# A cap on loads under way, more room for weights, and a table of importance in the planned start of an attention and mixing kernel

## The chip, the cores and the metric

The kernel runs on one NeuronCore of a Trainium2 chip. The metric is the device time of one execution in microseconds (us). TensorE (PE) multiplies matrices, VectorE (DVE), ScalarE (ACT) and GpSimd (POOL) work on tiles element by element, and SyncE (SP) issues all of the kernel's DMAs. Each engine works through its own list of instructions strictly in the order in which the program was written; semaphores hold an instruction back until what it needs is there.

## The reference

Two parts follow each other. The first is an attention over 8 heads: a pooled attention (queries, keys and values averaged over 4 positions, its result repeated 4 times) plus a local one (each position sees those less than 4 away). The second mixes tokens with two small weights and channels with two larger ones.

```python
q_d = q.reshape(B, H, Sd, 4, D).mean(axis=3)          # k_d, v_d likewise; B=8 H=8 S=576 D=64
out_up = np.repeat(sm_attn(q_d, k_d, v_d), 4, axis=2)
mask = np.abs(pos[:, None] - pos[None, :]) < 4
scores = np.where(mask, scale * q @ k.T, -1e9)
out_local = softmax(scores) @ v
x = (out_up + out_local)                              # as [B, S, 512]
h = relu(x.T @ w_tok1) @ w_tok2                       # tokens: 576 -> 256 -> 576
u = x + h.T
return u + relu(u @ w_ch1) @ w_ch2                    # channels: 512 -> 1536 -> 512
```

The weights arrive as 64-bit floating-point numbers, everything else as 32-bit ones.

## The kernel before

**Tiling.** The 8 batches are worked through one after another. Per batch, the 576 positions are cut into five tiles (four of 128, one of 64) for attention and the first token product, and into two halves of 256 and 320 positions for what follows. The stages and the names that the profile shows are these. Pooled attention, twice per batch for two halves of the heads: `sd` (scores), `pd` (exponentials), `td` and `ptd` (transposed), `ad` (times the summed values `vd`), `od` (the result). Local attention, per position tile: `sc` (scores), `P` (exponentials), `pT` and `pt` (transposed), `av` (times the values), `x` (the tile of the sum). The pooled result enters the local product as extra rows: twelve small DMAs copy `od` into the rows of `vw` that lie below the loaded values (L515), and `av` multiplies with the whole of `vw`. Then the mixing: `xh` (x in two parts), `t1` (the first token product, five pieces, shown as `t<-xh,W`), `hid` (its positive part), `t2` (the second one, four pieces per half, shown as `t<-ident,x` and `t<-W,hid`), `u`, its largest absolute value `um`, and `uh` (u scaled, in two half-precision parts). Last the channel products: `c<-uh,CW` with C1, `h`, and `c<-h,CX` with C2. Each takes three matmuls for every pair of parts, since numbers are kept in two parts.

**Weights.** A weight in 64 bits is loaded as it is and turned into 32 bits on the chip by `to_f32`: a step on ACT (L211), two on POOL (L214, L217) and one on DVE (L222), all in place in the loaded tile except the last, which for C1 and C2 writes the final tile. C1 and C2 have twelve tiles each, W (the two token weights) nine pieces. The DVE step ends the reading of a loaded piece (`(name, "read", i)`), and the next piece that uses the same buffer is loaded after it. C1's pieces have six buffers (`cw`), W's five (`h`, which later hold the channel products' intermediate results). C2's first four loads use the four `qk` buffers, once batch 0's five local tiles have been transposed, and the next four the `vw` buffer, once the last `av` is done.

**Order.** From the third batch on, and for the channel products of all but the first, the order is written out by hand (the loops at the end). The start, up to the end of batch 0 and the first scaled half of batch 1, is put in order by a planner, `drive`. Each stream of work (a Python generator) says before each step which engine it needs, for how long, and what must be made first. The planner keeps a clock for each engine and one for the loads (230 bytes per ns, and 2 us to land), takes the step that can start earliest, advances the clocks, and lets the stream write its instructions. Among steps on the same engine that can start within `PATIENCE` (0.15 us) of the earliest it takes the first stream in the list. Where PE would be idle in the plan, `keep_busy` puts in at most eight filler matmuls (`busy`). The planned times set only the order of the instructions; on the chip they wait for semaphores alone.

**Loads of batch 0.** `load` (L383) issues the four `qk` tiles ahead of the planner. `load_v` (L398) issues the six `vr` tiles at its first step, `weight_loads` (L230) one piece of W or C1 per step, `load_w` (L420) the two halves of `vw`. All of these go on SyncE's queue, in the planned order, and nothing limits how many are under way.

## Time and profile before

| | |
|---|---|
| median of 3 runs | 970.06 us (966.67 to 973.64) |
| the profiled execution | 967.52 us |
| its span, first to last instruction | 965.7 us |
| PE busy | 911.2 us (94%) |
| DVE, ACT, POOL busy | 425.8, 302.6, 205.5 us |
| mean granted TensorE clock | 0.973 |
| moved by DMA | 71.67 MB, 74 GB/s over the span |

The profile is of one execution. Its page gives the busy time of each engine, the span in 40 slices (a digit is the busy share of a slice in tenths), the DMA queues, the chain of work that ended last, and the costliest groups of instructions. A row of the timeline reads: start, length, engine, line, operation, output <- inputs, shapes and count, and in brackets how long the engine was idle ahead of it and what ended that. `issue` means that the engine waited for nothing that the profile shows. `SPq` is SyncE issuing a DMA. Queue q1 carries the kernel's own DMAs, q8 and q14 the engines' instructions.

### The profile page before, as it was taken

What the parts mean: (1) busy time and instruction counts of PE and PEld (TensorE: products, weight loads), DVE (VectorE), ACT (ScalarE), POOL (GpSimd) and SP (SyncE); (2) the same over time, 40 slices, a digit from 0 to 9 for tenths busy, and PEclk for the clock granted to TensorE, in tenths of its full rate; (3) what the DMA queues carried; (4) which work ended last, traced back from release to release, by engine and by line L of the source; (5) the groups of instructions that cost most, each with busy time, mean ns of one, the idle gap of its engine ahead of it and who ended that gap; (6) DMA issues with size and microseconds to landing.
All of it is one profiled execution on the core that took longest, in us unless ns stands there. A gap on an engine that the chain in (4) does not pass through costs nothing.

```text
span 965.7 us, 29160 instructions
## 1 busy us (share of the span) xinstructions
PE 911.2 (94%) x13142; PEld 698.3 (72%) x13150; DVE 425.8 (44%) x982; ACT 302.6 (31%) x675; POOL 205.5 (21%) x301
## 2 busy tenths in 40 slices
PE   6678899999989999999999999999999999999998
PEld 3545576777867777777877777777877778777876
DVE  4676786426343254334443255324443254333221
ACT  2354455214232142223332141322432142322110
POOL 4399960320222002300122002300113000000000
PEclk9597999999999999999999999999999999999999
DMA  9581630620242012500243002500124000000000
GB/s 261 190 288 54 222 73 15 178 74 26 64 144 55 15 30 78 170 8 21 56 133 76 14 27 81 171 1 28 52 90 123 7 23 21 18 1 22 18 12 28
DMA packets 31756, 71.67 MB, mean 74 GB/s; under 512 B 3808, under 2 KB 16608, under 8 KB 31008
## 3 DMA queue, kind: packets, MB, share of 16 engines
q1 hardware_dynamic: 31632, 69.81, 24.0%
q8 instruction: 103, 1.69, 0.8%
q14 instruction: 21, 0.17, 0.1%
HBM read 58.00 MB, written 9.44 MB: 70 GB/s over the span
## 4 chain that ended last, share of the span: by engine, by line
PE 76%; DVE 10%; POOL 4%; ACT 3%; issue 3%; DMA 2%; SPq 1%; ACTq 0%; POOLq 0%; DVEq 0%
PE c L115 51%; PE t L115 11%; PE av L569 3%; PE td L486 2%; PE ad L501 2%; PE t L633 2%; PE pT L556 2%; PE sc L533 1%; DVE r L550 1%; ACT pd L478 1%; DVE uh L679 1%; DMA vr<-in_vr_dram 1%; DVE P L545 1%; DVE mx L544 1%; PE sd L466 1%
## 5 line engine op out<-in xcount | busy, mean ns | idle before, releaser
L115 PE MATMUL c<-uh,CW 128*128 128x256 f16 (+1 forms) x2304 | 305.8, 287 | 1.9 <-DVE h L756 1.6
L115 PE MATMUL c<-h,CX 128*128 128x256 f16 (+1 forms) x2304 | 306.0, 287 | 1.6 <-issue 1.4
L115 PEld LDWEIGHTS <-CW 128*128 128x128 f16 x2304 | 217.3, 98 | 69.3 <-issue 14.1
L115 PEld LDWEIGHTS <-CX 128*128 128x128 f16 x2304 | 216.6, 98 | 62.6 <-issue 3.1
L756 DVE SCALAR_TENSOR_TENSOR h<-c,h 128x256 f16<-128x256 f32 (+1 forms) x192 | 87.6, 457 | 186.7 <-ACT h L754 186.3
L754 ACT ACTIVATE h<-c 128x256 f16<-128x256 f32 (+1 forms) x192 | 78.7, 410 | 227.0 <-PE c L115 226.8
L412 POOL TENSOR_TENSOR vr<-vr 128x256 f32<-128x256 f32 x48 | 37.4, 780 | 381.4 <-DMA vr<-in_vr_dram 373.0
L782 DVE SCALAR_TENSOR_TENSOR u<-c,io,u 128x256 f32<-128x256 f32 (+1 forms) x64 | 32.9, 514 | 117.2 <-PE c L115 117.1
L115 PE MATMUL t<-W,hid 128*128 128x256 f32 (+1 forms) x384 | 69.6, 317 | 1.8 <-DVE W L242 1.7
L115 PE MATMUL t<-xh,W 128*128 128x512 f32 (+1 forms) x240 | 68.8, 422 | 2.2 <-DVE xh L611 2.2
L437 POOL TENSOR_TENSOR qs<-qk 128x288 f32<-128x288 f32 x56 | 40.7, 727 | 113.4 <-DMA qk<-in_qk_dram 109.8
L658 ACT COPY u<-t 128x256 f32<-128x256 f32 (+1 forms) x64 | 25.5, 398 | 118.1 <-PE t L115 97.3
L660 DVE TENSOR_REDUCE umx<-t 128x1 f32<-128x256 f32 (+1 forms) x64 | 29.3, 458 | 70.5 <-ACT u L658 69.1
L115 PEld LDWEIGHTS t<-W,hid 128*128 128x128 f32 x384 | 55.0, 195 | 4.4 <-DVE W L242 1.9
L115 PEld LDWEIGHTS t<-xh,W 128*128 128x128 f32 (+1 forms) x240 | 44.0, 194 | 13.4 <-DVE xh L611 2.7
L611 DVE TENSOR_TENSOR xh<-x,xh 128x512 fp32r<-128x512 f32 (+1 forms) x40 | 30.4, 765 | 52.9 <-ACT xh L609 52.9
L569 PE MATMUL av<-vw,pt 47*32 47x64 f32 x2304 | 37.9, 226 | 7.2 <-DMA vw<-od 3.7
L569 PEld LDWEIGHTS av<-vw,pt 47*32 47x32 f32 x2304 | 28.1, 107 | 19.8 <-issue 8.0
L574 ACT COPY x<-av 128x512 f32<-128x512 f32 (+1 forms) x40 | 23.3, 584 | 55.0 <-PE av L569 50.8
L547 ACT ACTIVATE P<-P 128x304 f32<-128x304 f32 (+1 forms) x40 | 18.1, 456 | 64.7 <-DVE P L545 64.2
L677 ACT ACTIVATE uh<-u,us 128x256 f16<-128x256 f32 (+1 forms) x64 | 29.6, 525 | 27.7 <-DVE us L121 18.7
L533 PE MATMUL sc<-qk 64*32 64x38 f32 x2304 | 31.1, 212 | 4.4 <-issue 2.6
(107 smaller groups left out, 849.2 us busy)
## 6 DMA issues: line engine op xcount, KB each, us to landing
qk<-in_qk_dram SPq DMA_DIRECT2D x32, 579.0 KB
vr<-in_vr_dram SPq DMA_DIRECT2D x48, 256.0 KB
vw<-in_vw_dram SPq DMA_DIRECT2D x16, 702.0 KB
C_raw<-in_c_dram SPq DMA_DIRECT2D x16, 512.0 KB
out_dram<-u SPq DMA_DIRECT2D x32, 160.0 KB
C_raws<-in_c_dram SPq DMA_DIRECT2D x8, 512.0 KB
out_dram<-u SPq DMA_DIRECT2D x32, 128.0 KB
vw<-od SPq DMA_DIRECT2D x96, 24.0 KB
```

Source lines behind the costliest of these rows:

```text
L115: nc.tensor.matmul(ps, lhs(a), rhs(c), start=first and i == 0, stop=last and i == 2, **kw)
L412: nc.gpsimd.tensor_add(t[:, 0:2], t[:, 0:2], t[:, 2:4])
L437: nc.gpsimd.tensor_add(two, x[:, :, 0:2], x[:, :, 2:4])
L533: nc.tensor.matmul(ps[QB * j:QB * j + QB, par, WB * hp:WB * hp + WB], st.qk[hp][p, QB * g:QB * g + QB], st.qk[hp][p, S + QB * g:S + QB * g ...
L569: nc.tensor.matmul(ps[QB * j:QB * j + QB, par, D * hp:D * hp + D], pt[p, hp, QB * j:QB * j + QB], st.vw[p, g, D * COLUMN[hp]:D * COLUMN[hp ...
L611: nc.vector.tensor_tensor(xh[:, 1], xf(t), xh[:, 0].bitcast(F32), ALU.subtract)
L658: nc.scalar.copy(u, ps)
L660: nc.vector.tensor_reduce(umx[ch][:, c:c + 1], ps, axis=AX.X, op=ALU.max, apply_absolute_value=True)
L677: nc.scalar.activation(t[:, 0], st.u[ch][c], AF.Copy, scale=s)
L754: nc.scalar.activation(ht[:, 0], ps, AF.Relu)
L756: nc.vector.scalar_tensor_tensor(ht[:, 1], ps, 0.0, ht[:, 0], ALU.max, ALU.subtract)
L782: nc.vector.scalar_tensor_tensor(us[c], banks[c], io, us[c], ALU.mult, ALU.add)
```

## The change

Five things change, all of them in the planned start.

The loads of batch 0 (`qk`, `vr`, `vw`, and the W and C1 pieces that wait for no buffer) ask `room` first. While the bytes issued and not yet known to have landed, with the new load's, exceed 1.7 million, `room` takes the oldest load and issues a DMA of one word out of its tile into a small tile `seen`. SyncE can issue that DMA only when the load has landed, so what comes behind it on SyncE waits too. The planner's clocks move on to that load's planned arrival.

The last four of W's nine pieces get four buffers of their own (`wr`), so none of W's loads waits for another piece to be read. The space comes from the scratch for descriptors written by software, set to 1024 bytes.

Each stream gets a name (its group's letter and a number) and a place in `ORDER`. Among the steps on the earliest step's engine within `PATIENCE`, the planner now takes the one that stands first in `ORDER`. In SyncE's case the names that matter at the start are L1 (`vr`), L2 (W), L3 (`vw`), L4 (C1) and L5 (C2).

The six `vr` loads of batch 0 become six steps, and batch 1's five become five, instead of one step for all; batch 1's first still waits for the mixing of batch 0.

The steps of the second token product wait for all four of its weight pieces by name, and the copies of `od` for both of its halves, as the order among them is no longer fixed.

```diff
+ORDER = ("C5 m1 C2 C0 U0 A6 T0 A0 U1 W0 W6 W5 M3 W3 A2 M2 C8 A4 m3 L1 W4 L5 U2 M0 A3 C9 D9 A1 Q0 S0 D11 C7 D4 "
+         "a2 C11 m0 D10 a1 W8 P0 W1 W7 L0 m2 D8 h0 a5 D0 M1 W2 a4 D5 L4 H0 C10 C3 a6 A5 L2 C6 D7 a0 C4 D2 a3 "
+         "C1 P1 D1 D6 D3 L3 ").split()
+UNDER_WAY = 1.7e6
...
+    def room(nbytes):
+
+        while told[0] < len(sent) and sum(x[1] for x in sent[told[0]:]) + nbytes > UNDER_WAY:
+            t, _, at = sent[told[0]]
+            nc.sync.dma_start(seen[0:1, told[0]:told[0] + 1], t)
+            told[0] += 1
+            clock["S"] = max(clock["S"], at)
+            now[0] = max(now[0], at)
+
+    def arriving(tile, nbytes):
+        at = fetched(nbytes)
+        sent.append((tile, nbytes, at))
+        return at
...
-        items = [[g, next(g, None), 0.0] for g in streams]
+        items = [[g, next(g, None), 0.0, -ORDER.index(name)] for name, g in streams]
...
-            best = next(x for x in some if x[0] <= best[0] + PATIENCE and (x[0] == best[0] or x[1][1][0] == best[1][1][0]))
+            best = max((x for x in some if x[0] <= best[0] + PATIENCE and x[1][1][0] == best[1][1][0]),
+                       key=lambda x: x[1][3])
...
-            yield step("S", 0.1, *([(name, "read", i - BUFS[tag])] if i >= BUFS[tag] else []))
-            raws[i] = T([src.shape[0], 2 * n], U32, tag, f"{name}{i}_raw")
+            late = i >= BUFS[tag] and name == "C1"
+            yield step("S", 0.1, *([(name, "read", i - BUFS[tag])] if late else []))
+            raws[i] = T([src.shape[0], 2 * n], U32, "wr" if i >= BUFS[tag] and not late else tag, f"{name}{i}_raw")
+            if not late:
+                room(src.shape[0] * n * 8)
             nc.sync.dma_start(raws[i], src)
-            made[name, "raw", i] = fetched(src.shape[0] * n * 8)
+            made[name, "raw", i] = arriving(raws[i][0:1, 0:1].bitcast(F32), src.shape[0] * n * 8)
...
+            if b == 0:
+                room(579e3)
             nc.sync.dma_start(t, qk[b, hp])
...
+            if st.b == 0:
+                room(262e3)
             nc.sync.dma_start(ts[i], vr[st.b, kc, two].rearrange("p (r c) -> p r c", r=4))
...
-        if early:
-            yield step("S", 0.1, *([("mixed", 0)] if st.b else []))
         for i in range(early):
+            yield step("S", 0.1, *([("mixed", 0)] if st.b and i == 0 else []))
             fetch(i)
...
         for par in range(2):
+            if st.b == 0:
+                room(0.7e6)
             nc.sync.dma_start(st.vw[64 * par:64 * par + 1 + WB].rearrange("p g c -> p (g c)"), vw[st.b, par])
...
+        make(("od", b, two), e)
         if two == 1:
-            yield step("S", 0.2, ("vw", b), at=e)
+            yield step("S", 0.2, ("vw", b), ("od", b, 0), at=e)
...
-                    e = yield step("P", 1.2, ("W", "y", NT + 3), ("hid", b),
+                    e = yield step("P", 1.2, *(("W", "y", NT + i) for i in range(4)), ("hid", b),
...
-        streams = [x for k in "LMCTWUDSAmPHaQh" for x in group[k]]
+        streams = [(f"{k}{i}", x) for k in "LMCTWUDSAmPHaQh" for i, x in enumerate(group[k])]
...
-    nc = _bacc.Bacc("TRN2", target_bir_lowering=False, num_devices=1)
+    nc = _bacc.Bacc("TRN2", target_bir_lowering=False, num_devices=1, dynamic_dma_scratch_size=1024)
```

More of the change, by code (lines that the diff above doesn't have):

```diff
@@ L50, in tile_ups_attention_mixer @@
     psum = ctx.enter_context(tc.tile_pool(name="psum", bufs=1, space=bass.MemoryType.PSUM))
-    BUFS = dict(cw=6, h=5, w=3, xh=3, x=5, u0=4, u1=8, uh0=4, uh1=4, qk=4, qd=1, vw=1, vd=1, pt=2, od=1, sm=10, ev=4, nm=4, qs=1, sc=20)
+    BUFS = dict(cw=6, h=5, w=3, xh=3, x=5, wr=4, u0=4, u1=8, uh0=4, uh1=4, qk=4, qd=1, vw=1, vd=1, pt=2, od=1, sm=10, ev=4, nm=4, qs=1, sc=20)
     SLOTS = dict(gg=2, m=3, g=1, w=3)
@@ L145, in fetched @@
         return clock["D"] + 2.0
+    sent, told = [], [0]
+    seen = sb.tile([1, 64], F32, name="seen")
+    def room(nbytes):
[9 more added lines that the diff above has]
+        return at
     def keep_busy(n):
@@ L382, in load @@
             t = T([128, S + KW], F32, "qk", f"qk{b}_{hp}")
+            if b == 0:
+                room(579e3)
             nc.sync.dma_start(t, qk[b, hp])
             st.qk.append(t)
-            st.at.append(fetched(579e3))
+            st.at.append(arriving(t[0:1, 0:1], 579e3))
         return st
@@ L397, in fetch @@
             ts[i] = T([128, 4, 128], F32, tag, f"vr{st.b}_{i}")
+            if st.b == 0:
+                room(262e3)
             nc.sync.dma_start(ts[i], vr[st.b, kc, two].rearrange("p (r c) -> p r c", r=4))
-            arrives[i] = fetched(262e3)
+            arrives[i] = arriving(ts[i][0:1, 0, 0:1], 262e3)
         early = {0: 6, 1: 5}.get(st.b, 0)
-        if early:
-            yield step("S", 0.1, *([("mixed", 0)] if st.b else []))
         for i in range(early):
+            yield step("S", 0.1, *([("mixed", 0)] if st.b and i == 0 else []))
             fetch(i)
@@ L419, in load_w @@
         for par in range(2):
+            if st.b == 0:
+                room(0.7e6)
             nc.sync.dma_start(st.vw[64 * par:64 * par + 1 + WB].rearrange("p g c -> p (g c)"), vw[st.b, par])
-        make(("vw", st.b), fetched(1.4e6))
+            at = arriving(st.vw[64 * par:64 * par + 1, 0, 0:1], 0.7e6)
+        make(("vw", st.b), at)
     def pool_q(st, hp):
@@ L502, in pooled @@
                                          st.vd[p, kc, 2 * two + odd], start=kc == 0, stop=kc == 2)
-        if two == 0:
+        if not hasattr(st, "od"):
             st.od = T([128, 2, 3, 2, D], F32, "od", f"od{b}")
```

## The prediction, made before the result was known

> **What bounds the kernel now.** I read the page's slices first, then a table of stretches cut where the chain of waits changes its character, then the waits, then SyncE's issues.
>
> ```profile
> span 965.7 us, 29160 instructions
> ...
> POOL 4399960320222002300122002300113000000000
> ```
> ```profile
> 18.50:25.75 7.25, 0.00 (x1) 0.00 (x0) 0.00 (x0) 0.65 (x3) 0.76 (x1) 0.66 0.94 211
> 25.75:41.00 15.25, 11.33 (x419) 9.27 (x421) 8.55 (x23) 4.32 (x9) 3.35 (x5) 0.50 0.62 214
> 41.00:66.00 25.00, 19.52 (x398) 13.35 (x398) 22.15 (x37) 14.51 (x32) 21.84 (x20) 0.86 0.62 206
> 66.00:86.00 20.00, 13.91 (x57) 7.76 (x59) 12.28 (x22) 9.93 (x19) 18.65 (x18) 0.82 0.43 167
> 86.00:111.00 25.00, 19.24 (x111) 13.98 (x112) 17.48 (x38) 9.48 (x20) 23.41 (x21) 0.80 0.49 159
> 111.00:169.00 58.00, 54.05 (x1128) 41.94 (x1128) 45.26 (x101) 33.56 (x72) 25.55 (x33) 0.97 0.26 69
> 169.00:227.00 58.00, 56.80 (x551) 44.66 (x538) 19.85 (x44) 11.51 (x23) 16.57 (x29) 1.00 0.41 115
> ```
>
> Columns: length, then busy time of PE, PE's weight loads, DVE, ACT, POOL; the granted clock; the DMA share; GB/s. From 111 us on PE is the limit: 110.9 busy of 116 us up to 227, where the planned part ends. Everything this change touches lies ahead of that. So I ask one question: when does the first product with a channel weight (`c<-uh,CW`) start? What moves that start moves the end, if PE stays as full behind it. Before it, three stages: PE does nothing from 18.5 to 25.75; until 41 every engine is mostly idle (POOL 3.35 of 15.25); from 41 to 111 POOL decodes weights, 63.9 busy of 70 us.
>
> ```profile
> 18.50 7.25 issue
> ...
> 41.17 2.15 DMA vw<-od
> ```
> ```profile
> ACT ptd L490 <- PE td L486: 12.7, 3, 10.5
> ...
> POOL C_raw L217 <- ACT C_raw L211: 9.3, 2, 8.0
> ```
>
> The first row is from the chain of waits: PE has no releaser, it waits for its own instructions. Behind it ACT sits 10.5 us on `ptd`, and POOL 8.0 us on an ACT step that stands behind `ptd` in ACT's order. That is why decoding starts late.
>
> ```profile
> DMA packets 1593, 4.43 MB, mean 341 GB/s; under 512 B 173, under 2 KB 173, under 8 KB 1581
> ```
> ```profile
> DMA packets 281, 1.84 MB, mean 167 GB/s; under 512 B 41, under 2 KB 41, under 8 KB 214
> ```
> ```profile
> q1 hardware_dynamic: 184, 1.27, 97.9%
> ```
> ```profile
> q8 instruction: 1, 0.02, 2.8%
> ```
> ```profile
> DMA packets 106, 1.47 MB, mean 113 GB/s; under 512 B 26, under 2 KB 26, under 8 KB 26
> ```
>
> These are rows of the DMA view for 0 to 13 us, for 13 to 24 us, for 15 to 22.7 us (the loads' queue is the only one in it), for 22.7 to 26 us (here PE's instruction packet appears), and for 132 to 145 us, where batch 1's `vw` load runs alone. 341 GB/s falls to 167 at 13 us, when `vw` comes up, and `vw` alone gets 113. PE's fetch is served when `vw` has drained. So the early queue is long mostly because of one slow load.
>
> **The change, part by part.**
>
> *The order of the loads.* In the table of importance the work items for `vr` (L1), C2 (L5), C1 (L4), W (L2) and `vw` (L3) stand in this order; L3 is the very last entry. Each wait in `room` moves SyncE's planned clock past all of them, so that they tie, and then importance decides. Walking the code: `qk` four times, `vr` with C1's first pieces between, then C1's later pieces (which need no `room`) in turn with the W pieces, and `vw` after all of them. Before:
>
> ```profile
> 8.87 0.98 SPq L420 DMA_DIRECT2D vw<-in_vw_dram  x2
> ...
> 36.01 8.68 SPq L515 DMA_DIRECT2D vw<-od  x12
> 44.80 4.71 SPq L230 DMA_DIRECT2D C_raw<-in_c_dram  x2
> ...
> 60.43 0.33 SPq L230 DMA_DIRECT2D W_raw<-in_w_dram  x1
> ```
> ```profile
> qk<-in_qk_dram SPq DMA_DIRECT2D x32, 579.0 KB
> vr<-in_vr_dram SPq DMA_DIRECT2D x48, 256.0 KB
> vw<-in_vw_dram SPq DMA_DIRECT2D x16, 702.0 KB
> C_raw<-in_c_dram SPq DMA_DIRECT2D x16, 512.0 KB
> ```
> ```profile
> W_raw<-in_w_dram SPq DMA_DIRECT2D x4, 288.0 KB
> ```
>
> Ahead of `vw` there will be 4 x 579 + 6 x 256 + 12 x 512 + W (4 x 288, and by the code's shapes 4 x 256 and 128) = 12,300 KB, 12.6 MB. At 341 GB/s that is 37 us; `vw` itself, 1.44 MB, takes 8.6 us at 167 or 12.7 at 113. It lands at 46 to 50 us; I take 48. The twelve copies of `od` into it stand behind it on SyncE: before 8.68 us, and 2.15 to land, so they are complete at 59 us instead of 46.8 (36.01 + 8.68 + 2.15). This part alone costs 12 us on the way to `av`. It gives back that decoding need not wait.
>
> *Room for all nine W pieces.* The last W load went at 60.43, since each of the last four waited for a buffer. Now none waits. POOL's bill:
>
> ```profile
> L217 POOL TENSOR_SCALAR C_raw<-C_raw 128x512 bf16<-128x512 f32 x14 | 21.4, 1527 | 2.3 <-ACT C_raw L211 1.3
> L214 POOL TENSOR_SCALAR C_raw<-C_raw 128x512 uint32<-128x512 uint32 x13 | 13.3, 1020 | 1.0
> ...
> L217 POOL TENSOR_SCALAR W_raw<-W_raw 128x288 bf16<-128x288 f32 (+2 forms) x6 | 7.2, 1196 | 0.5
> ...
> L214 POOL TENSOR_SCALAR W_raw<-W_raw 128x288 uint32<-128x288 uint32 (+2 forms) x6 | 4.0, 662 | 0.5
> ```
>
> Twelve C1 tiles at 2.55 us and nine W at 1.86 make 47.4 us; the six `vr` sums add about 7. Begun at 10 to 17 us it is done at 64 to 71, where the stretches above show POOL full until 111 with C2 mixed in. What is late next: the C1 loads seven to twelve wait for a buffer, piece i for the decoding of piece i-6. By then POOL owes six `vr` and six C1, 22 us, so the twelfth can go near 33 us: inside the 37. C2's loads need the `qk` buffers, free only when the local tiles are transposed; that comes later than now, but 12 x 2.55 us from about 66 still ends ahead of 111.
>
> *The cap.* `room` makes SyncE wait for the oldest load by copying one of its words to `seen`. Some 28 such copies at the 0.33 us that the W row shows for an issue are 9 us of SyncE's time, spread over the 48 us up to `vw`, while the loads themselves are in flight. Each copy is also a reader that the in-place decode must wait out: at least the 2.15 us to land, and up to 5.0 more if it queues behind 1.7 MB at 341 GB/s. That delays the first decodes (10 becomes 17 above), not their rate. For PE's fetch: 1.7 MB drain in 5.0 us, against the wait it has now. Before, the stall is 7.25 us; after, between 0 and about that, I take 4. It is hidden in any case: `od` was ready at 36 us with the whole stall, and `vw` lands at 48.
>
> By the Trainium skill (DMA: Bandwidth & Descriptors, section "Queues, rings and completion order") a DMA engine takes turns between queue rows packet by packet, so a fetch on its own row should not see how deep the loads' row is; then the cap buys PE nothing. The trace speaks against it, with a fetch served only after the slow load, but shows no time of asking.
>
> *The tie-break by the table, the split waits, the early buffers.* These reorder work inside 0.15 us of planned time. No row prices it; between -3 and +3 us, taken as 0. The waits on four W pieces and on both `od` halves name work that is done earlier anyhow. The smaller descriptor scratch costs nothing: the loads are all in the SyncE queue.
>
> **From `vw` to the first product.**
>
> ```profile
> 65.31 0.65 PE L569 MATMUL av<-vw,pt 47*32 47x64 f32 x32
> ...
> 82.56 0.38 PE L633 MATMUL t<-ident,x 128*128 128x128 f32 x2
> ...
> 90.72 0.95 PE L115 MATMUL t<-W,hid 128*128 128x256 f32 x6
> ...
> 110.94 1.47 PE L115 MATMUL c<-uh,CW 128*128 128x256 f16 x12
> ```
> ```profile
> 204.46 1.65 PE L115 MATMUL t<-xh,W 64*128 64x512 f32 x6
> ...
> 210.94 0.38 PE L633 MATMUL t<-ident,x 128*128 128x128 f32 x2
> ...
> 218.76 0.94 PE L115 MATMUL t<-W,hid 128*128 128x256 f32 x6
> ...
> 227.17 0.38 PE L115 MATMUL c<-uh,CW 128*128 128x256 f16 x2 [0.28 <-ACT uh L677]
> ```
>
> Batch 0 runs among the decoding, batch 1 without: these are the two bounds of each step. (a) `od` copies complete to last `av`: 18.5 us now; three at the least, an estimate from five tiles of 0.65 us and no wait. I take 8: 67 us. (b) Last `av` to first `t2`: 17.3 now; 4.8 in batch 1 from its last `t1` product. I take 10: 77. (c) `t2` of the first half: 9.1 and 8.8: 86. (d) From there to the first product: 19.3 now, 7.5 in batch 1. I take 11: 97 us. All taken values lie toward batch 1's end, since the W and C1 decoding that filled these stretches is done by then and C2's alone is left. The bounds add up to 83 and 123 us.
>
> So 110.9 - 97 = 14 us gained. PE behind it: 110.9 of 116 us busy, so the shift should hold. The profiled execution took 967.52 us, its span 965.7; the median of the three runs, 970.06, is 2.5 above. 967.5 - 14 = 953.5, against the median **956 us**; own range 946 to 966, a start at 87 to 107.
>
> In 25.75 to 41 us, after PE's idle 7.25, the granted clock is 0.50. The skill (TensorE: Matmul & The Clock Gate, "HAM oscillation") says that idle gaps above about 3.4 us halve the clock; the trace agrees. PE will now idle before `vw`, and `av` and `t1` would then start at half rate, some 3 us by an estimate: 959.
>
> **Rivals.**
>
> *Moved, not shortened* (0.20): `av` comes late and (a), (b), (d) take the middle of their bounds, 10.8, 11 and 13.4: 59 + 44 = 103, or a little more if C2 crowds DVE as now (17.48 of 25 us): 103 to 114. For it: DVE and POOL were both busy, not POOL alone. Time 962 to 973.
>
> *The cap does nothing for the fetch* (0.10): a fetch that takes turns with the loads, as that page has it, was then late for another cause, and the 7.25 us stay. ACT and POOL lose the 8.0 us again, decoding ends near 79, W is late for `t2` by 6: 103 us, so 962.
>
> *The last place of `vw`* (0.20, slower): SyncE works strictly in order, so if the C1 buffers are freed at today's pace, W and `vw` stand behind them. Today the last W load goes at 60.4 us. If `vw` lands beyond 62 (62 + 49 = 111), or at 50 with steps at today's lengths, the product starts later than 110.9: at 50, 61 + 18.5 + 17.3 + 9.1 + 19.3 = 125, 14 us lost: 984. For it: the idle stretch before 41 us was not DVE's alone, and POOL has no spare. Against: loading no longer waits for PE's stall.
>
> **Numbers.** Forecast 0.50. A difference under 1%, 9.7 us, is about what runs spread by here (966.67 to 973.64) and can't be told from none. Faster is below 960.4: 0.43 of the forecast's 0.50 and 0.06 of the others, 0.49. Slower is above 979.8: 0.16 of the last rival and 0.02 of the first, 0.18. The rest, 0.33, is the same. Range 944 to 980: leaves out 0.04 below and the 0.16 to 0.18 of late `vw`.
>
> **What would show it.** Right: `vw` issued after the last W, near 37 us; `od` copies at 48 to 57; POOL 15 or more of 25.75 to 41 us busy; first `c<-uh,CW` at 92 to 103; the stall at 18.5 shorter. Wrong: SyncE waiting on DVE's reads of C1 beyond 45 us; `av` beyond 75; a first product at 110 or later; or PE idle between it and the second product, waiting for C2.

## The result, and the profile after

The changed kernel takes 975.21 us in the median (972.9 to 978.54) against 969.94 (964.45 to 973.64) for the kernel before: a ratio of 1.0071, 95% interval 1.0054 to 1.0088. That is a small loss, under the 1% that the prediction took as its bound, but clear of zero, where a gain of 14 us was forecast. The profiled execution took 974.83 us, with a span of 973.0 against 965.7.

From the page: the span, and POOL's row of the 40 slices.

```profile
span 973.0 us, 29215 instructions
...
POOL 4659770051123003300113003300113000000000
```

The table of stretches, cut as in the prediction (columns: length, busy time of PE, PE's weight loads, DVE, ACT and POOL, granted clock, DMA share, GB/s):

```profile
18.50:25.75 7.25, 6.21 (x225) 4.57 (x228) 6.40 (x15) 3.16 (x7) 6.84 (x10) 0.79 0.79 247
25.75:41.00 15.25, 10.63 (x307) 6.67 (x298) 13.22 (x26) 7.05 (x16) 12.32 (x14) 1.00 0.81 198
41.00:66.00 25.00, 12.01 (x262) 8.85 (x261) 7.71 (x17) 8.21 (x18) 10.18 (x13) 0.66 0.58 166
66.00:86.00 20.00, 12.79 (x113) 6.98 (x111) 14.89 (x20) 11.35 (x23) 18.74 (x17) 0.83 0.68 251
86.00:111.00 25.00, 18.08 (x101) 13.45 (x102) 18.98 (x37) 10.42 (x21) 20.31 (x19) 0.80 0.14 42
111.00:169.00 58.00, 51.92 (x933) 40.49 (x932) 49.67 (x108) 30.85 (x67) 27.84 (x36) 0.91 0.39 115
169.00:227.00 58.00, 54.98 (x674) 41.98 (x660) 15.21 (x30) 12.73 (x25) 15.16 (x25) 0.92 0.39 104
```

The start is better: PE's idle 7.25 us from 18.5 us on are gone, and POOL is busy 12.32 us up to 41 instead of 3.35. But from 41 to 66, where POOL did 21.84 us before, it now does 10.18. And behind 111 us PE is no longer full: 51.92 and 54.98 against 54.05 and 56.80, at a lower clock.

SyncE's issues in the timeline show how the middle came about:

```profile
32.26 0.41 SPq L452 DMA_DIRECT2D vw<-in_vw_dram  x1
32.73 0.58 SPq L160 DMA_DIRECT2D seen<-W_raw  x1
33.35 0.40 SPq L452 DMA_DIRECT2D vw<-in_vw_dram  x1
33.86 0.58 SPq L160 DMA_DIRECT2D seen<-W_raw  x1
34.48 0.40 SPq L257 DMA_DIRECT2D W_raw<-in_w_dram  x1
40.01 0.58 SPq L160 DMA_DIRECT2D seen<-vw  x1
...
45.70 0.59 SPq L160 DMA_DIRECT2D seen<-vw  x1
...
46.95 9.37 SPq L549 DMA_DIRECT2D vw<-od  x12
...
56.86 1.24 SPq L160 DMA_DIRECT2D seen<-W_raw  x2
...
65.94 0.38 SPq L257 DMA_DIRECT2D W_raw<-in_w_dram  x1
```

`vw` is not the last load: it goes ahead of W's third piece. From 34.48 on SyncE stands behind one-word copies out of `vw`, which can be issued only when its two halves have landed (40.0 and 45.7), then issues the twelve copies of `od` for 9.37 us. W's last piece is loaded at 65.94, where the kernel before had it at 60.43 and the prediction near 37. POOL pays for it. Here are the waits up to 120 us (total, times, longest), and the three for W in POOL's timeline:

```profile
POOL W_raw L238 <- DMA seen<-W_raw: 14.7, 3, 8.1
PE av L603 <- DMA vw<-od: 13.0, 4, 7.4
POOL C_raw L238 <- DMA seen<-C_raw: 12.6, 1, 12.6
```
```profile
40.25 0.60 POOL L238 TENSOR_SCALAR W_raw<-W_raw 128x256 uint32<-128x256 uint32 x1 [1.83 <-DMA seen<-W_raw]
...
45.63 0.42 POOL L238 TENSOR_SCALAR W_raw<-W_raw 128x256 uint32<-128x256 uint32 x1 [4.77 <-DMA seen<-W_raw]
...
60.37 0.94 POOL L238 TENSOR_SCALAR W_raw<-W_raw 128x256 uint32<-128x256 uint32 x2 [8.08 <-DMA seen<-W_raw]
```

SyncE issues a copy only once its load has landed, so these pieces are there; POOL may not decode them in place before the one-word copies out of them have been carried out. The first two copies were issued at 32.73 and 33.86, each behind one half of `vw`, and POOL goes on 7.5 and 11.8 us later. The longest wait is for copies that SyncE could issue only at 56.86, after those of `od`. The wait of 12.6 us is the one for the first decode; 7.2 us of it pass without the copies too, for the load itself (e1 below). PE's timeline has the steps of the prediction: the last `av`, the first `t2`, the first product with what stands just ahead of it, and the first one of batch 1.

```profile
74.08 1.18 PE L603 MATMUL av<-vw,pt 47*32 47x64 f32 x64
...
92.23 0.63 PE L667 MATMUL t<-ident,x 128*128 128x128 f32 x2
...
118.01 0.61 PE L353 MATMUL C_sum<-CX 128*128 128x128 bf16 x4 [1.65 <-DVE CX L246]
118.41 2.76 PE L121 MATMUL c<-uh,CW 128*128 128x256 f16 x12
...
238.33 1.47 PE L121 MATMUL c<-uh,CW 128*128 128x256 f16 x12
```

The first product starts 7.5 us later than before (110.94), batch 1's 11.2 later (227.17), the end of the span 7.3. The row ahead of it is a sum over a tile of C2, for which PE waits until DVE has decoded the tile (`CX`).

### The profile page after: what moved, and what is told of

Its sections match the earlier page's. It is cut to its first block, busy times and chain, and to the rows that moved or that the text cites. A ratio compares the mean times of both kernels' runs of the same rounds, so it can differ in the third digit from the quotient of the medians.

```text
span 973.0 us, 29215 instructions
## 1 busy us (share of the span) xinstructions
PE 910.1 (94%) x13150; PEld 697.7 (72%) x13150; DVE 430.0 (44%) x982; ACT 303.5 (31%) x675; POOL 203.9 (21%) x301
## 4 chain that ended last, share of the span: by engine, by line
PE 76%; DVE 9%; DMA 5%; ACT 4%; SPq 2%; POOL 2%; issue 1%; ACTq 0%; POOLq 0%; DVEq 0%
PE c L121 51%; PE t L121 11%; PE av L603 3%; PE td L519 2%; PE t L667 2%; PE pT L590 2%; PE ad L534 2%; DMA vw<-od 2%; PE sc L567 1%; ACT pd L511 1%; DMA seen<-W_raw 1%; SPq L549 1%; DVE P L579 1%; DVE r L584 1%; DVE uh L713 1%
## 5 line engine op out<-in xcount | busy, mean ns | idle before, releaser
L470 POOL TENSOR_TENSOR qs<-qk 128x288 f32<-128x288 f32 x56 | 42.3, 755 | 118.7 <-DMA qk<-in_qk_dram 114.8
L603 PE MATMUL av<-vw,pt 47*32 47x64 f32 x2304 | 40.1, 235 | 21.8 <-DMA vw<-od 19.4
L603 PEld LDWEIGHTS av<-vw,pt 47*32 47x32 f32 x2304 | 29.5, 111 | 34.7 <-issue 16.1
L121 PEld LDWEIGHTS t<-xh,W 128*128 128x128 f32 (+1 forms) x240 | 43.2, 191 | 12.7 <-issue 2.2
L711 ACT ACTIVATE uh<-u,us 128x256 f16<-128x256 f32 (+1 forms) x64 | 29.9, 524 | 28.0 <-DVE us L127 17.4
L713 DVE SCALAR_TENSOR_TENSOR uh<-u,us,uh 128x256 f16<-128x256 f32 (+1 forms) x64 | 31.6, 538 | 5.4 <-ACT uh L711 5.3
```

The costliest lines, as they stand in the source:

```text
L121: nc.tensor.matmul(ps, lhs(a), rhs(c), start=first and i == 0, stop=last and i == 2, **kw)
L470: nc.gpsimd.tensor_add(two, x[:, :, 0:2], x[:, :, 2:4])
L603: nc.tensor.matmul(ps[QB * j:QB * j + QB, par, D * hp:D * hp + D], pt[p, hp, QB * j:QB * j + QB], st.vw[p, g, D * COLUMN[hp]:D * COLUMN[hp ...
L711: nc.scalar.activation(t[:, 0], st.u[ch][c], AF.Copy, scale=s)
L713: nc.vector.scalar_tensor_tensor(t[:, 1], st.u[ch][c], s, t[:, 0], ALU.mult, ALU.subtract)
```

## The experiments

The first product with C1, and batch 1's, cut each run in three: the start, the stretch between them, and the rest of the span. This table serves all experiments; "order of before" means that the planner breaks ties as in the kernel before. Times in us from the profiles, ratios with their 95% intervals.

| kernel | ratio to before | first product | stretch to batch 1's | rest |
|---|---|---|---|---|
| before | 1 | 110.9 | 116.2 | 738.5 |
| after | 1.0071 [1.0054, 1.0088] | 118.4 | 119.9 | 734.7 |
| *order of before* | | | | |
| e3, cap alone | 1.0132 [1.0102, 1.0161] | 127.2 | 114.8 | 737.4 |
| e4, short rows of `vw` | 0.9928 [0.9901, 0.9955] | 108.3 | 115.3 | 737.3 |
| e6, room for W alone | 0.9999 [0.9984, 1.0013] | 116.9 | 114.4 | 737.2 |
| e12, e4 and a later price | 0.9918 [0.9891, 0.9945] | 113.5 | 110.9 | 739.8 |
| e16, e4 and two queues | 1.0043 [1.0019, 1.0067] | 114.1 | 115.5 | 739.5 |
| *order by the table* | | | | |
| e1, no copies | 1.0005 [0.9974, 1.0036] | 109.7 | 121.6 | 741.2 |
| e2, no cap | 1.0006 [0.9990, 1.0023] | 111.3 | 120.9 | 739.3 |
| e5, table alone | 1.0072 [1.0048, 1.0097] | 106.1 | 127.8 | 738.0 |
| e7, copies of `qk`, `vw` | 1.0014 [0.9988, 1.0040] | 110.9 | 122.9 | 737.0 |
| e8, copies of the rest | 1.0019 [0.9998, 1.0040] | 114.6 | 120.4 | 735.6 |
| e9, e5 and a later price | 1.0039 [1.0010, 1.0068] | 110.9 | 121.4 | 739.2 |
| e11, after, short rows | 1.0101 [1.0068, 1.0134] | 117.5 | 123.8 | 738.4 |
| e13, e1, short rows, later price | 0.9980 [0.9959, 1.0000] | 100.6 | 128.5 | 735.8 |
| e14, e5 and two queues | 1.0057 [1.0025, 1.0089] | 107.6 | 126.7 | 734.9 |
| e15, after, two queues | 1.0050 [1.0027, 1.0073] | 118.7 | 121.2 | 736.3 |
| e17, after, cap of 3.4 MB | 1.0003 [0.9982, 1.0023] | 110.6 | 120.6 | 736.4 |
| e18, e5, C2 in turn | 1.0166 [1.0144, 1.0188] | 106.8 | 138.5 | 736.2 |
| e19, after, C2 in turn | 1.0183 [1.0147, 1.0219] | 112.3 | 134.9 | 736.5 |

Each row is one profile. The rest, which no edit here touches, still spreads over 6.5 us (734.7 to 741.2), so a few us between two rows are not told apart. The stretch is 111 to 116 us in every kernel with the order of before, and 120 to 139 in every one with the table. None of these kernels leaves out any of the computation; some leave out copies into `seen`, which nothing reads.

### The parts of the change

**e1: the changed kernel without its copies.** The plan, and so the order on every engine, is kept.

```diff
-            nc.sync.dma_start(seen[0:1, told[0]:told[0] + 1], t)
```

> The changed kernel with every instruction in the same planned order, but the one-word copies into `seen` are not issued, so nothing on SyncE waits for a load to land and no decode waits for a copy. Theory 1 (the copies are the loss: they hold the loads back on SyncE and the in-place decode behind `vw`): the first channel product moves from 118 us to 105 or earlier and the time to 955 to 964. Theory 2 (the planned order is the loss: `vw` late, C1 and W behind it): 972 to 978, as the changed kernel.

Measured 970.52 us, between the two theories; the first product at 109.70, not 105. The copies cost 4.7 us of time and 8.7 of the first product. POOL is busy 19.30 of the 25 us from 41 on instead of 10.18. PE's waits for its own instructions, 3.6 us in the changed kernel up to 41 us (1.04, 1.64, 0.95), are 11.9 here (2.00, 1.43, 1.61, 5.75, 1.15). So the cap does shorten the fetch stall, as meant. In the changed kernel the stall is hidden: `od` is done at 39.4 us and `vw` has landed at 45.7. Here it is not: `od` is done at 42.80 and its copies go at 42.83.

**e2: no cap.** `UNDER_WAY = 1.7e9`; then the plan has no waits for landing loads either.

> The changed kernel with the cap lifted to 1.7 GB, so that neither the copies nor the jumps of the planner's clocks happen; room for all W pieces and the table stay. Theory 1: 955 to 966, near the run without the copies. Theory 2, if the table is what is bad: 972 to 978; if it is the jumps, that put `vw` behind C1 and W, about the kernel before, 966 to 972. PE's stall on its own instructions near 18 us should be back at about 7 us if the cap had removed it.

Measured 971.08 us, which is in the range for the jumps of the planner's clocks; but e1, which has the jumps, takes the same time. So it is the copies and not the plan made with them that costs. PE's waits for its own instructions up to 41 us are 8.5 us here, the longest 4.82.

**e3: the cap and its copies alone,** in the kernel before (the parts of the diff with `room`, `arriving` and `seen`).

> The kernel before with the cap and its copies alone. Theory 1: slower than before by 5 to 12 us, 975 to 982, POOL waiting for the copies as it does in the changed kernel. Theory 2: within 3 us of before. PE's stall at 18.5 us falls from 7.25 to 4 or less if the cap does what the prediction took it for, and stays if a fetch does not queue behind the loads.

Measured 981.84 us, in the range of Theory 1. POOL does wait for copies (21.0 us up to 90, against 27.3 in the changed kernel), but another wait is longer. PE's timeline and SyncE's:

```profile
44.52 0.61 PE L327 MATMUL C_sum<-CW 128*128 128x128 bf16 x4 [36.44 <-DVE CW L240]
```
```profile
71.06 9.03 SPq L542 DMA_DIRECT2D vw<-od  x12
```

The plan that the cap makes in this order puts a sum over the first decoded C1 tile ahead of the pooled attention. PE stands there for 36.4 us, `od` is done only at 71.0 instead of 36.0, and its copies go at once. So e3 measures that order and not the price of the copies, and PE's fetch stall can't be read from it. The changed kernel has the table and the room for W as well; which of the two keeps this from happening there was not tested.

**e4: `vw` in short rows,** in the kernel before: batch 0's load is cut into ten DMAs with rows of at most 4 KB, where two have rows of 18 KB.

```diff
+            for g in range(0, NG, GP if st.b == 0 else NG):      # GP = 4
-            nc.sync.dma_start(st.vw[64 * par:64 * par + 1 + WB].rearrange(...), vw[st.b, par])
+                nc.sync.dma_start(st.vw[64 * par:64 * par + 1 + WB, g:g + n].rearrange(...),
+                                  vw[st.b, par][:, 256 * g:256 * (g + n)])
```

> The kernel before with batch 0's `vw` load cut into ten DMAs of rows of 4 KB or less in place of two of rows of 18 KB. If the long rows make the load slow (113 to 167 GB/s where others reach 341), 13 to 24 us now moves over 300 GB/s, PE's stall of 7.25 us falls under 3, and the time falls by 3 to 8 us, 962 to 967. If the slowness has another cause, such as the few partitions that it writes: no change, 968 to 972.

Measured 962.40 us, 0.7% faster than before and in the theory's range, and not a part of the change at all. The DMA view for 13 to 24 us (167 GB/s before), and PE's waits for its own instructions in the timeline:

```profile
DMA packets 809, 2.25 MB, mean 204 GB/s; under 512 B 163, under 2 KB 163, under 8 KB 808
```
```profile
20.88 0.34 PE L505 MATMUL ad<-vd,ptd 48*64 48x65 f32 x8 [1.11 <-issue]
...
27.62 0.47 PE L537 MATMUL sc<-qk 64*32 64x38 f32 x23 [4.04 <-issue]
...
35.29 1.28 PE L537 MATMUL sc<-qk 64*32 64x38 f32 x96 [4.06 <-issue]
```

The stretch moves 204 GB/s, not the 300 expected. The stall of 7.25 us is 1.11, but two of 4 us come later: up to 41 us all such waits add up to 9.2 us, against 10.2 before. What comes earlier is `od`, whose copies go at 31.33 instead of 36.01. The slow load was rightly named in the prediction, and its shape pays where the cap does not. The edit changes the length of the rows and the number of DMAs together; which of them counts was not tested.

**e5: the table alone,** in the kernel before (the diff's parts in `drive`, and the split waits that come with them).

> The kernel before with the table of importance alone (and the waits by name that go with it), no cap, no buffers for W. Since the planned order without copies came out at the time of before, two halves may cancel. If the table is a gain that the room for W spoils: 960 to 966 here. If the table is a loss that the room for W makes good: 973 to 978. If both are neutral: 966 to 972.

Measured 974.93 us, 6 more than before, although its first product is 4.8 us earlier: the stretch behind it is 127.8 us instead of 116.2. That is the range for a table whose loss the room for W makes good: e2 has both, with the `vr` loads in steps, and a ratio of 1.0006.

**e6: room for all W pieces alone** (the diff's `wr` buffers and the smaller scratch).

> The kernel before with four buffers of their own for W's last pieces alone. The prediction gave this part most of its gain, since W's late pieces held up the second token product: 960 to 966. If the pieces still come late because SyncE issues them behind the `od` copies, or because POOL's order decides and not their landing: 966 to 972.

Measured 968.03 us, no difference. W's last load goes at about 33 us instead of 60.43, and nothing gets faster; in the profile the first product comes 6.0 us later.

**e7 and e8: half of the copies each.** In the changed kernel, e7 issues only those out of `qk` and `vw`, e8 only those out of `vr`, W and C1.

```diff
+            if size in (579e3, 0.7e6):         # e8: not in
                 nc.sync.dma_start(seen[0:1, told[0]:told[0] + 1], t)
```

> The changed kernel in the same planned order, with copies into `seen` of `qk` and `vw` words alone: SyncE still waits for `vw` to land (40 and 46 us), but no in-place decode waits for a copy. If SyncE standing behind `vw` is the loss: 973 to 977 as the changed kernel, first channel product near 118 us. If the decode waiting for copies is the loss: 967 to 971, near 110 us.

> The counterpart: copies of `vr`, W and C1 words alone, so the decodes and the `vr` sums wait for copies, and SyncE does not wait for `vw`. If SyncE standing behind `vw` is the loss: 967 to 971. If the decode waiting for copies is the loss: 973 to 977, POOL waiting 20 us or more for `seen` ahead of 66 us.

Measured 970.87 and 969.81 us: neither differs from e1 by more than the measurement can tell. The first product moves by 1.2 and 4.9 us, against 8.7 with both. So it takes both: copies out of `vw` that hold SyncE, and copies out of the W and C1 pieces that come late and hold POOL. In either run alone, what the expectation named as the loss is not there.

### Where the copies cost

**e11: the changed kernel with e4's short rows.**

> The changed kernel, with batch 0's `vw` load cut into ten loads with rows of 4 KB or less instead of two with rows of 18 KB. Theory (the one-word copies of W's first pieces queue behind the long rows of `vw`, and POOL starves): POOL's wait for `seen<-W_raw`, 14.7 us in three before, falls below 6, and the time from 975 to 969 to 972. Rival (the copies cost as steps of SyncE and as readers that every in-place decode waits out, wherever they stand): the waits shrink by less than half and the time stays at 973 to 977.

Measured 979.35 us, above both ranges, and POOL's wait is little shorter:

```profile
POOL W_raw L239 <- DMA seen<-W_raw: 11.7, 3, 6.6
```

The theory fell: the longest wait is again for copies issued after those of `od`, and the other two take 5.0 us together instead of 6.6. So the length of `vw`'s rows is the smaller part of these waits. The result is even 4 us worse than the changed kernel, mostly in the stretch (123.8); its cause was not pursued.

**e17: a cap of 3.4 MB.**

```diff
-UNDER_WAY = 1.7e6
+UNDER_WAY = 3.4e6
```

> The changed kernel with a cap of 3.4 MB instead of 1.7 MB. With 1.7 MB 975.2, with no cap at all 971.1, with the plan of 1.7 MB but no copies 970.5. Theory (each one-word copy costs SyncE about 0.6 us and lands behind what is under way; a copy made later finds its load already there): fewer copies, waits of POOL for `seen<-W_raw` and `seen<-C_raw` below half of 27.3 us, 970 to 973. Rival (a copy that lands behind twice as many bytes delays its reader twice as long): waits of 27 us or more, 974 to 980.

Measured 968.58 us, no different from before, and 6.6 better than with 1.7 MB; the first product is back at 110.6. POOL's waits for copies up to 120 us:

```profile
POOL vr L442 <- DMA seen<-vr: 12.8, 1, 12.8
...
POOL C_raw L238 <- DMA seen<-C_raw: 3.6, 1, 3.6
```

For W and C1, which the expectation names, 3.6 us are left of 27.3, well below half, and none for W; a wait of 12.8 us for the first `vr` copy is new. The time is below the range of either theory. The number of bytes allowed under way was thus the costly choice of the change, and with twice as many the change is worth nothing either way.

### Where the table costs

In kernels with the table PE has a gap at batch 1's `av`, and a low clock behind it. Stretches of the kernel with the table alone (e5), then short ones of the kernel before, where the same `av`, begun at 150.57, goes on at 152.93 us:

```profile
164.00:168.00 4.00, 1.06 (x9) 0.54 (x6) 3.12 (x8) 0.72 (x1) 0.00 (x0) 0.84 0.05 12
168.00:172.00 4.00, 0.46 (x14) 0.25 (x14) 0.00 (x0) 0.00 (x0) 0.00 (x0) 0.50 0.16 41
172.00:176.00 4.00, 2.35 (x79) 1.78 (x85) 1.37 (x4) 2.03 (x4) 0.00 (x0) 0.50 0.09 25
176.00:180.00 4.00, 3.99 (x161) 3.13 (x142) 2.51 (x5) 2.40 (x4) 0.00 (x0) 0.50 0.02 4
```
```profile
151.00:152.00 1.00, 0.00 (x0) 0.00 (x0) 1.00 (x3) 0.46 (x2) 0.00 (x0) 1.00 0.10 25
...
154.00:155.00 1.00, 1.00 (x6) 0.57 (x4) 0.02 (x1) 0.94 (x2) 0.00 (x0) 0.50 0.21 52
...
156.00:157.00 1.00, 1.00 (x38) 0.48 (x37) 0.00 (x0) 0.28 (x1) 0.00 (x0) 0.50 0.00 0
```

With the table PE does 1.5 us of work in 8 and then runs 8 us at half clock; before, it loses 2 us and runs some 3 us at half clock. Added up in steps of 2 us from 140 to 195 us, PE's idle time is 10.0 us in e5 and 3.1 before, and what its work loses to a clock below 1.00 is 3.7 and 1.7 us: 8.9 of the 11.6 us by which the stretch of e5 is longer. The same idle time is 1.0 to 3.1 us in every kernel with the order of before, and 5.9 to 13.4 in every one with the table. SyncE's timeline of the kernel before, of e5 and of the changed kernel shows when batch 1's `qk` loads and `od` copies go:

```profile
93.93 5.66 SPq L383 DMA_DIRECT2D qk<-in_qk_dram  x4
...
145.48 8.78 SPq L515 DMA_DIRECT2D vw<-od  x12
```
```profile
121.60 2.07 SPq L388 DMA_DIRECT2D qk<-in_qk_dram  x4
...
165.22 8.56 SPq L521 DMA_DIRECT2D vw<-od  x12
```
```profile
111.86 2.15 SPq L412 DMA_DIRECT2D qk<-in_qk_dram  x4
...
164.93 8.55 SPq L549 DMA_DIRECT2D vw<-od  x12
```

Batch 1's `od` copies come 20 us later than before. Four theories of what makes the gap were tried.

**e9: a later planned price,** in e5. The plan takes 3.0 us from the end of `od` to its copies' landing; here it takes 11.0.

```diff
-            make(("full", b), e, 3.0)
+            make(("full", b), e, 11.0)
```

> The kernel before with the table alone, and with the planner told that the twelve copies of `od` take 11.0 us, not 3.0. The table alone measured 975, 6 above the kernel before, with a first product 5 us earlier; in its profile PE waits 6.9 us and its weight loads 3.2 us for `vw<-od` in batch 1 (2.0 and 2.1 before). Theory (the table may place batch 1's `av` right behind copies that the plan thinks are over; PE, in order, stands there): these waits fall to 4 us or less in all, and the time to 967 to 971. Rival (the table's loss lies in the order of the other streams): 973 to 977 whatever the waits are.

Measured 973.26 us, in the rival's range, though the intervals of e5 and e9 overlap. PE's and its weight loads' waits for `vw<-od` in batch 1 fell from 10.1 to 5.6 us, but a gap with other waits stays at the same place.

**e12 and e13: the same price with short rows,** in the order of before (e12) and in the changed kernel without copies (e13).

> The kernel before with `vw` of batch 0 in rows of 4 KB or less (alone: 962.4) and with the planned price of the `od` copies at 11.0 instead of 3.0. If the plan's price is what costs PE its waits for `vw<-od` in batch 1, also in the order of before (2.0 and 2.1 us there), 958 to 961. If that price only matters together with the table: 961 to 964. If the later `av` pushes other steps back: above 964.

> The changed kernel without its copies (alone 970.5), with `vw` of batch 0 in rows of 4 KB or less and the price of the `od` copies at 11.0. Sum of the parts if both theories hold (split worth 6, price worth 5): 958 to 961. If the price is worth nothing: 963 to 966. If the split pays only by PE's instruction fetch in the order of before (here the stall is 5.75 us at 32 us, and `od` is bound by `vw`): 966 to 971.

e12 measured 962.02 us, as e4: the price is worth nothing there, or only together with the table. But its profile has the `od` copies of batch 1 at 158.93, 13 us later than before, and the shortest stretch of all, with PE busy 9.04 of the 10 us from 161 on. Late copies alone do not make the gap. e13 measured 966.62 us, in the last range of its expectation (the reason given there, that `vw` binds `od` in e1, is not what e1 shows): it has the earliest first product (100.6) and loses all of that lead in a stretch of 128.5 us.

**e14, e15 and e16: the copies of `od` on two queues.** Every second one is issued by ACT, in batch 1 of e5 (e14), and in batches 0 and 1 of the changed kernel (e15) and of e4 (e16).

```diff
+                eng = nc.scalar if n % 2 and b == 1 else nc.sync        # e15, e16: b < 2
-                nc.sync.dma_start(st.vw[64 * par + 1 + WB:64 * par + KB, ...
+                eng.dma_start(st.vw[64 * par + 1 + WB:64 * par + KB, ...
```

> The kernel before with the table alone (974.9), and with every second of the twelve `od` copies of batch 1 issued by ACT instead of SyncE. The plan is the same to the last step. With the table alone the copies are issued for 8.6 us from 164.9 us on, PE waits for `vw<-od` 10 us in all, is busy 3.48 of 10 us from 161 to 171 us, and is granted a clock of 0.53 from 171 to 181. Theory (the gap at batch 1's `av`, and the low clock behind it, are the table's loss): the issue halves to about 4.3 us, the waits fall by 4 us or more, the clock behind them stays above 0.8, and the time comes to 967 to 971. Rival (the loss lies in the order of other work, and PE only meets it here): 973 to 977 with the waits gone.

> The changed kernel (975.2) with every second of the `od` copies of batches 0 and 1 issued by ACT. In batch 0 SyncE is held 9.37 us by the copies, with five W loads behind them. Theory (SyncE's issue time of the copies is on the way to both `av` blocks and holds the W loads): W's last load, issued at 65.9, goes 4 us earlier, the first `c<-uh,CW` comes 2 to 5 us before 118.4, batch 1's gap shrinks by 4 us or more; 966 to 970. Rival (the one-word copies set the pace of SyncE, whatever else it issues): the first product moves by less than 1.5 us, and only batch 1's gap is won: 971 to 974.

> The kernel before with batch 0's `vw` in rows of 4 KB or less (962.4) and every second of the `od` copies of batches 0 and 1 issued by ACT. PE waits 4.1 us for `vw<-od` in batch 1 there. If the issue time of these copies is on PE's way in any order: 957 to 961. If the order of before hides it: 961 to 964.

e14 measured 971.99 us, short of the theory's range and not told apart from e5; from 164 to 172 us PE still does 3.6 us of work in 8, and the clock behind is 0.50. By the medians the issue time of the copies is about half of the loss (2.9 of 6.2 us), by the ratios a fifth; the intervals leave both open. e15 measured 972.86, with the first product no earlier (118.7) and a stretch no shorter (121.2): the rival's range, but not told apart from the changed kernel either. e16 was 10 us worse than e4. Its timeline:

```profile
31.37 4.86 ACTq L520 DMA_DIRECT2D vw<-od  x6
...
36.28 0.67 ACT L212 ACTIVATE C_raw<-C_raw 128x512 f32<-128x512 f32 x1 [6.10 <-DMA vw<-od]
...
38.30 5.74 SPq L520 DMA_DIRECT2D vw<-od  x6
```

ACT does no other work while it issues; decoding waits for it 6.10 us. SyncE's half goes only at 38.30, behind C1 and W loads issued from 35.59 on, where all twelve went at 31.33 in e4.

**e18 and e19: C2's tiles in turn.** In the table C2's tiles 0 to 3 stand low, and batch 1's `qk` loads need the buffers of these.

```diff
-... M0 A3 C9 D9 A1 Q0 S0 D11 C7 D4 a2 C11 m0 D10 ... D7 a0 C4 D2 a3 C1 P1 D1 D6 D3 L3
+... M0 A3 C9 D0 A1 Q0 S0 D1 C7 D2 a2 C11 m0 D3 ... D7 a0 C4 D8 a3 C1 P1 D9 D10 D11 L3
```

> The kernel before with the table alone (974.9), but with the twelve entries of the table for C2's tiles (D0 to D11) in ascending order at the places that they hold. In the table D9, D11, D4, D10 and D8 stand ahead of D0 and D3 is last but one; batch 1's `qk` loads take over the buffers of C2's tiles 0 to 3, so that SyncE issues them at 121.6 us behind C2's last four loads, where the kernel before issues them at 93.9, ahead of those. Batch 1's `od` copies then go at 165 us against 145, when batch 0's products no longer fill PE. Theory (that is the table's loss): the `qk` loads go ahead of C2's last four loads, at 95 to 108 us, the `od` copies at 145 to 157, the stretch from the first `c<-uh,CW` to batch 1's product falls from 127.8 us to 114 to 120, and the time to 963 to 970. Rival (another place of the table costs it, and this only moves the wait): the stretch stays at 122 or more, 972 to 977.

> The changed kernel (975.2) with the table's entries for C2's tiles in ascending order. Its `qk` loads of batch 1 go at 111.9 us, its `od` copies of batch 1 at 164.9, and from the first `c<-uh,CW` (118.4) to batch 1's product are 119.9 us, where kernels with the order of before have 114 to 116. Theory (the table's loss and the cap's add up): the first product stays within 2 us of 118.4, the stretch falls to 114 to 117, the time to 969 to 972. Rival (at this late first product the order no longer matters): 973 to 977.

Both theories and both rivals fell: 983.42 and 984.51 us. In e18 the loads and the copies do go early, as expected:

```profile
107.56 3.64 SPq L388 DMA_DIRECT2D qk<-in_qk_dram  x4
...
153.35 0.74 SPq L425 DMA_DIRECT2D vw<-in_vw_dram  x2
154.15 15.29 SPq L521 DMA_DIRECT2D vw<-od  x12
```
```profile
161.00:171.00 10.00, 4.05 (x134) 2.80 (x131) 1.64 (x8) 1.02 (x2) 0.00 (x0) 0.73 0.37 64
171.00:181.00 10.00, 7.02 (x159) 4.68 (x153) 3.64 (x5) 6.16 (x11) 6.79 (x11) 0.75 0.60 233
```

Yet the gap is longer. `od` of batch 1 is done at 147.4 us, but batch 1's `vw` is loaded only at 153.35 (141.95 in e5), just ahead of the copies into it, which take 15.29 us to issue instead of 8.56: the wait for `qk` has become one for `vw`. And batch 0's second products (`c<-h,CX`), which start at 155.64 us in e5, start at 181.58 here, each behind the scaling of its C2 tile. One list of twelve names moved the whole plan, so the test did not isolate what it meant to.

## Why the prediction was wrong

**What held.** The landing of `vw` (45.7 us against 46 to 50) and that of the `od` copies came out: 46.95 + 9.37 + 2.2 to land is 58.5 us, 59 forecast. For `vw` this was luck. It went ahead of seven W and five C1 pieces, so 7,948 KB stood ahead of it and not 12,300; they moved at about 270 GB/s from 3 to 32.3 us, not 341; and `vw` then took 13.4 us, where the bounds were 8.6 and 12.7. The upper bound rests on the 113 GB/s of a window of 13 us that batch 1's `vw` fills only in part: from 133 to 142.5 us it moves 1.44 MB, 151 GB/s. The stall fell as the cap was meant to make it, to 3.6 us in all (4 forecast), and it was hidden, as said: `od` was done 6.3 us before `vw` had landed. The Trainium skill (DMA: Bandwidth & Descriptors, "Queues, rings and completion order") has each DMA engine take turns between queue rows, packet by packet, from which the prediction drew that a fetch on its own row should not feel how deep the loads' row is. These two kernels with the same order, 3.6 us with the copies and 11.9 without, speak against that here.

**Where the miss lies.** The first product came 21.4 us after the 97 forecast, and the time was 19 us above the forecast. By the prediction's own steps, measured in the changed kernel and in e1, which has the same order without the copies:

| step | taken | after | e1 |
|---|---|---|---|
| `od` copies complete | 59 | 58.5 | 53.7 |
| (a) to the last `av` done | 8 | 16.8 | 11.8 |
| (b) to the first `t2` | 10 | 17.0 | 17.4 |
| (c) first half of `t2` | 9 | 8.4 | 7.1 |
| (d) to the first product | 11 | 17.8 | 19.7 |

**The first step that failed: "That delays the first decodes (10 becomes 17 above), not their rate."** The first decode does come at 17 us (16.95). But the copies go on setting the rate: POOL waits 14.7 us for them between 38 and 60 us and does 10.18 of 25 us of work from 41 on, where 21.84 were done before. The prediction saw that a copy might queue up to 5.0 us; it missed that the copies out of W's first pieces would be issued right behind `vw`, and that SyncE, held until `vw` had landed and then by the `od` copies, would issue the next copies at 56.9 and W's last piece at 65.9. In the table this is 4.8 us of the `od` copies and 5.0 of (a), and without the copies (e1) the loss against the kernel before is gone. "Now none waits" for a buffer was true and of no use; e6 shows that W's buffers were not the limit before either.

**The second: (b) and (d) had the wrong ends of their bounds, copies or not.** They were taken near batch 1's, since decoding would be over by 64 to 71 us. POOL is done with W's last piece at 86.5 us, and in e1 at 77.1; the first `t2` starts some 3 us after DVE's last step on it in both (89.1 and 79.7). Both steps lie close to the lengths of before (17.3 and 19.3) in e1 as well, and together they are 13.8 us of the miss. In (d) DVE is busy 16.1 of 17.8 us (16.1 of 19.7 in e1), with C2's decoding, C1's scaling and `uh`, where it is busy 2.6 of 7.5 in batch 1 of the kernel before; PE stands behind it, as the row at 118.01 shows. (d) is 16.5 us or more in e2, e4, e13 and e17 too. That C2's decoding was left in (d) was written down, but no time was given to it. The first rival had named DVE and a start at 103 to 114 us, which is where e1's lies (109.7); with the copies the start is later than that. The 118.4 us are, nearly, the last rival's second form: `vw` at 50 with steps at today's lengths, 125. That rival gave 984, and 975 was measured. Its stated place, SyncE held by C1's buffers, is not what was seen.

**The third: what moves the first product's start moves the end, "PE as full behind it".** In the order of before this held within a few us: e3, e4, e6, e12 and e16 moved the start by 16.2, -2.7, 6.0, 2.5 and 3.1 us and the end of the span by 13.7, -4.8, 2.9, -1.6 and 3.4. With the table it does not: the stretch is 4 to 22 us longer, and among most of them the longer, the earlier it starts (100.6 and 128.5, 106.1 and 127.8, 109.7 and 121.6, 118.4 and 119.9). For the changed kernel the end moved by 7.3 us with a start moved by 7.5, but that is a stretch 3.7 us longer and a rest 3.8 shorter. Had the forecast of 97 us come true, e13 suggests what it would have brought: with a start at 100.6, 966.6 and not 956.

**A term that came out for another reason: the table "between -3 and +3 us, taken as 0".** Alone it costs 6 us (e5). With the room for W and the `vr` loads in steps it costs nothing (e2), though the room alone is worth nothing (e6); why the two make up for each other was not found. The table acts on every tie up to 227 us, and most of its cost in e5 lies around batch 1's `av`: PE idle for 6.5 of 8 us, then 8 us at a clock of 0.50. The Trainium skill has it that idle gaps above about 3.4 us halve the clock (TensorE: Matmul & The Clock Gate, "HAM oscillation"); these rows show the halving, but the kernel before shows it behind a gap of 2.0 us too.

**The sum as measured.** Order, room and table without the copies: 0 (e1, 1.0005). Copies at 1.7 MB: the remaining 4 to 7 us (e1, e2 and e17 against the changed kernel). The gain that was expected at the first product is not there, and the part of it that e1 has (1.2 us) is given back in the stretch.

**What stays open.** Which entries of the table lengthen the stretch. A planned price too low (e9) and the copies' issue time (e14) moved the median by 1.7 and 2.9 of 6.2 us, with intervals that overlap that of e5; the late `qk` loads (e18) were moved, but with so much else that the run decides nothing; e12 shows that late copies need not make a gap. It is shown that the loss is there, and that PE idles at batch 1's `av`. In e5 batch 0's first products are over by then, but 264 of the 288 matmuls of its second ones are still to come: they stand behind `av` in PE's order, and DVE is done with the C2 tiles for them only at 180.8 us. What would remove the gap is not shown.

The fastest kernels are e4 and e12, 0.7 to 0.8% under the kernel before, both without any part of the change.

## What to carry to other kernels

A wait placed in an issue queue that works in order holds everything behind it, and a copy used as a probe is also a reader: whoever rewrites its source in place waits until it has run, behind all that was queued before it. When a milestone is used to forecast the end, look at what stands in the limiting engine's order behind that milestone: with the table a start up to 10 us earlier brought batch 1's product no earlier than before. When bounds for a step are taken from two places, ask which engine sets it in each: here the decoding kept (d) near the longer bound with the copies and without. A slow load was worth reshaping here (e4, 0.7% faster), while rationing all loads cost 0.7%.

## What the runs showed of the hardware

- Two loads with rows of 18 KB move at 151 GB/s alone (133 to 142.5 us of the kernel before), and the stretch around batch 0's at 167; as ten loads with rows of 4 KB or less that stretch moves 204 GB/s, and the kernel gains 0.7% (e4).
- An idle PE of 2.0 us (151.0 to 152.9 in the kernel before) was followed by a granted clock of 0.50 from 154 to 157 us, while PE was busy.
- PE's waits for its own instructions up to 41 us were 11.9 us with no limit on the loads under way (e1) and 3.6 with one, at the same order of loads.
- ACT issued six copies of 24 KB in 4.86 us, in which it did no other work (e16).
- A copy of a single word costs SyncE about 0.6 us to issue; two that were issued behind halves of `vw` let POOL go on only 7.5 and 11.8 us later.
